# A long convolution with a routed expert: one stage's matmuls made with 128 moving columns instead of 256

## The chip, the cores and the metric

The kernel runs on one core of a Trainium2 chip. The metric is the device time of one execution in microseconds (us), of which the median of three runs is taken. Five engines work beside each other: PE (TensorE: matmuls, with its weight loads shown apart as PEld), DVE (VectorE), ACT (ScalarE), POOL (GpSimd) and SP (SyncE, which issues DMAs).

## What is computed

Two steps, for 8 sequences ("units" here, 0 to 7) of 6336 positions and 128 channels, all in float32:

```python
# step 1: causal convolution along the sequence, by Fourier transforms
Xf = np.fft.rfft(x, n=2*S, axis=1)
Hf = np.fft.rfft(h, n=2*S, axis=0)
y  = np.fft.irfft(Xf * Hf[None], n=2*S, axis=1)[:, :S, :]
# step 2: in each sequence the 128 positions with the highest score go through an expert
scores = np.einsum('bsd,d->bs', y, w_gate)
out = y.copy()
for b in range(B):
    top = np.argpartition(-scores[b], 128)[:128]
    xe = y[b, top]
    g = 1 / (1 + np.exp(-scores[b, top]))
    out[b, top] = xe + g[:, None] * (np.maximum(xe @ w1, 0) @ w2)
```

The change touches step 1 alone.

## The kernel before, in words

The sequence is cut as 50 x 128 (`N1` = 50, `N2` = 128), and the transform is done by matmuls against tables, in four stages for each unit:

- **a** (`stage_a`, matmuls on line 194): the products over the 50, out of the loaded input blocks; ACT or DVE copies the result to `reg[unit % 2]`. The two buffers of `reg` are `big` (even units) and `reg` (odd units).
- **b** (`stage_b`, matmuls through the helper `by_halves`, line 109): the products over the 128 (called n2), one for each of the 50 values of k. The 50 are taken in 13 chunks, `KCH`: twelve of 4 and one of 2. A chunk's weights `wt` come from HBM (`load_b`, tile `wbuf`, for units 6 and 7 partly `big`). The moving operand `rows_of(unit, k)` is 128 x 256 of `reg`: 128 pairs of neighbouring floats, each pair 100 floats behind the last. The results of four k fill a pair of PSUM banks (`pt`, 128 x 1024); there are two such pairs (`pairs`), used in turn. DVE multiplies them with the filter's spectrum (lines 276 and 282, two outputs, one of them in place of the input in `reg`), and POOL adds the parts (line 287).
- **c** (`stage_c`, line 300): the inverse products over the 128, 64 moving columns each, 64 matmul calls in one call of the stage; ACT copies them out to `half` (line 301).
- **d** (`stage_d`, line 320): the inverse products over the 50, 128 moving columns each, read out of `half` as 64 pairs of neighbouring floats, each pair 256 floats behind the last. ACT and DVE combine the results (lines 324, 329, 330), POOL multiplies them with the gate's weights (line 338), and SP sends them to HBM.

`by_halves` cuts a product by its 128 output rows: it issues two matmuls, one with weight columns 0 to 63 and one with 64 to 127, with the same moving operand, which write the partitions 0 to 63 and 64 to 127:

```python
for lo in range(0, n, 64):
    hi = min(lo + 64, n)
    nc.tensor.matmul(out[lo:hi], w[:, lo:hi], r, **k)
```

The order of all work is written out by hand (`manual_schedule`, the list `plan`). First come the filter and unit 0: stage a of both, then the "j" steps, which make the filter's spectrum (`stage_h`) and do stage b of unit 0. From then on two kinds of stretch alternate: c of unit u merged with b of unit u+1 (two calls of c, then two chunks of b, and so on; seven such stretches, of units 1 to 7 in b), and d of unit u merged with a of unit u+2. DVE's share of the search for the 128 best positions (`search`) is spread over both; for units 6 and 7 the experts follow at the end, whose products also go through `by_halves`, with 128 contiguous moving columns (line 645).

Of the kernel before, what the change touches and what calls it, by code (L numbers as in the profile page):

```python
# [33 lines left out]
def conv_moe(ctx, tc, x, h, w_gate, w1, w2, fa_d, wb_d, wc_d, at_d, tri_d, cst_d, outs):  # L34
# [19 lines left out]
    def pair():  # L54
        return turn(pairs)
# [8 lines left out]
    def wide(name):  # L64
        return tp.tile([128, 1024], F32, tag="t", name=name, bufs=5)
# [39 lines left out]
    def by_halves(out, w, r, **k):  # L105
        n = out.shape[0]
# [3 lines that stand above are left out]
# [115 lines left out]
    def rows_of(unit, k):  # L225
        return reg[(unit + 2) % 2].rearrange("p (j k t) -> p j k t", k=N1, t=2)[:, :, k]
# [33 lines left out]
    def stage_b(unit, c, tabs):  # L260
        wt, ht = tabs
        k0, kn = KCH[c]
        pt = pair()
        for k in range(kn):
            by_halves(pt[:, k * 256:k * 256 + 256], wt[:, k], rows_of(unit, k0 + k), start=True, stop=True)
        pt = pt[:, 0:kn * 256]
        rv = reg[unit % 2].rearrange("p (h a j k t) -> p h a j k t", h=2, a=4, k=N1, t=2)[:, :, :, :, k0:k0 + kn]
        tx = wide("tx")[:, 0:kn * 256]
        tv = tx.rearrange("p (h a j k t) -> p h a j k t", h=2, a=4, k=kn, t=2)
        if unit >= SINGLE:  # L270
            src = pt.rearrange("p (z r b x) -> p b z r x", r=2, b=2, x=32)
            for b in range(2):
                for w, dst in zip(ht, (rv, tv)):
                    o = dst.rearrange("p h a j k t -> p (h a) j k t")[:, 4 * b:4 * b + 4].rearrange("p a j k t -> p k a j t")
                    f = w[:, b].rearrange("p (z x) -> p z x", x=32).unsqueeze(2).broadcast_to([128, 2 * kn, 2, 32])
                    v.tensor_tensor(out=o, in0=src[:, b], in1=f, op=ALU.mult)
        else:
            src = pt.rearrange("p (k h a j t) -> p k h a j t", h=2, a=4, j=16, t=2)
            for w, dst in zip(ht, (rv, tv)):
                w = w.rearrange("p (k h j t) -> p k h j t", h=2, j=16, t=2)  # L280
                w = w.unsqueeze(3).broadcast_to([128, kn, 2, 4, 16, 2])
                v.tensor_tensor(out=dst.rearrange("p h a j k t -> p k h a j t"), in0=src, in1=w, op=ALU.mult)  # L282
        h = 4 if unit >= SINGLE else 2
        yv = reg[unit % 2].rearrange("p (h r j z) -> p h r j z", h=h, r=2, z=2 * N1)[:, :, :, :, 2 * k0:2 * (k0 + kn)]
        zv = tx.rearrange("p (h r j z) -> p h r j z", h=h, r=2, z=2 * kn)
        for r in range(2):
            g.tensor_tensor(out=yv[:, :, r], in0=yv[:, :, r], in1=zv[:, :, 1 - r], op=ALU.add if r else ALU.subtract)  # L287
# [525 lines left out]
    for s in plan:  # L813
        kind, unit = s[0], s[1]
# [30 lines left out]
        elif kind == "j":  # L845
# [12 lines left out]
            if early:  # L858
                spectra.append(join())
            stage_b(0, c, (tabs.pop(s)[0], [st[:, 0:n], st[:, n:2 * n]]))  # L860
            if join and not early:
                spectra.append(join())
            if s[2] < 8:
                load_x(16 + s[2])
            if s[2] in (2, 4, 6, 8):
                fold_to(15 + s[2] // 2)
        elif kind == "b":
            stage_b(*s[1:], tabs.pop(s))
            if unit == SINGLE and s[2] in (9, 11):
                load_x((unit + 2) * 8 + s[2] // 2 + 1)  # L870
# [161 lines left out]
```

## Time and profile before

| | |
|---|---|
| runs | 797.77, 797.80, 798.41 us; median 797.8 us |
| profiled execution | 804.7 us, of which the trace's span is 802.8 us |
| granted TensorE clock, mean | 0.983 of full speed |
| PE busy | 735.0 us (92%) |
| PEld busy | 643.2 us (80%) |
| DVE busy | 629.7 us (78%) |
| POOL busy | 551.3 us (69%) |
| ACT busy | 451.5 us (56%) |

"Busy" is the time in which at least one instruction of that engine is under way. A matmul call of float32 shows as two records of PE and two of PEld. Matmul records overlap, so the mean duration of one is longer than the step from one to the next; a step has to be worked out from the length of a row and the number of records in it. "The chain" is the work that ended last, followed back from the last instruction to what released each step.

### The profile page before, as it was taken

Reading aid. Unit: us, or ns where it says so; the run is one execution under the profiler, and the core shown is the slowest. Engines: PE = TensorE matmul, PEld = TensorE weight load, DVE = VectorE, ACT = ScalarE, POOL = GpSimd, SP = SyncE. Lnnn points to the kernel's source line nnn. Section 1 sums busy time; section 2 is a strip of 40 time slices with the busy share of each in tenths; the row PEclk is TensorE's granted clock in tenths of the full one; section 3 lists DMA queues with packets and bytes.
Section 4 is the critical chain, followed back from the end, with each engine's and each line's share of the span. In section 5 each row is a group of like instructions: output and inputs, shape, how many; then the busy total and the mean of one; then the engine's idle time right before and its main releaser. Section 6 shows DMA issues by size and latency. Waiting matters only on the chain.

```text
span 802.8 us, 39710 instructions
## 1 busy us (share of the span) xinstructions
PE 735.0 (92%) x17566; PEld 643.2 (80%) x17566; DVE 629.7 (78%) x1067; ACT 451.5 (56%) x965; POOL 551.3 (69%) x406
## 2 busy tenths in 40 slices
PE   6699979999999999999999999999999998888665
PEld 6675578888999878987889788889888888778554
DVE  5549956676767699999877898999668997975983
ACT  4687643365336546666456466655554666655562
POOL 0018928977797779877978698777885666722933
PEclk9889989999999999999999999999999999999989
DMA  7829816657865776578647774699478736521610
GB/s 268 259 83 329 267 55 215 208 166 233 261 216 160 231 261 215 155 219 273 229 126 230 256 259 123 193 331 327 126 224 267 253 110 183 171 65 31 205 54 17
DMA packets 82292, 157.64 MB, mean 196 GB/s; under 512 B 9366, under 2 KB 30088, under 8 KB 82120
## 3 DMA queue, kind: packets, MB, share of 16 engines
q1 hardware_dynamic: 81224, 154.05, 59.4%
q8 instruction: 138, 2.26, 1.1%
q0 software_dynamic: 896, 1.05, 0.5%
q14 instruction: 34, 0.28, 0.1%
HBM read 121.77 MB, written 33.29 MB: 193 GB/s over the span
## 4 chain that ended last, share of the span: by engine, by line
PE 65%; DVE 18%; issue 7%; DMA 5%; ACT 2%; POOL 1%; SPq 1%; another core or an unknown queue 0%; POOLq 0%; DVEq 0%; ACTq 0%
PE pb L300 23%; PE pt L109 17%; PE pb L320 10%; PE pt L194 10%; DVE tx L282 2%; DVE cmp L464 2%; PE pb L109 2%; PE pb L194 1%; PE pm L109 1%; DVE ss L354 1%; DVE st L329 1%; DVE st L330 1%; DMA out<-st 1%; ACT junk L477 1%; DVE st L251 1%
## 5 line engine op out<-in xcount | busy, mean ns | idle before, releaser
L301 ACT COPY half<-pb 114x512 f32<-114x512 f32 x224 | 147.0, 656 | 165.5 <-PE pb L300 161.1
L287 POOL TENSOR_TENSOR big<-big,tx 128x512 f32<-128x512 f32 (+1 forms) x104 | 132.0, 1302 | 77.5 <-DVE tx L282 68.0
L338 POOL TENSOR_TENSOR tm<-st,wg 114x1024 f32<-114x1024 f32 x56 | 133.8, 2392 | 63.4 <-DVE st L330 41.7
L287 POOL TENSOR_TENSOR reg<-reg,tx 128x512 f32<-128x512 f32 (+1 forms) x104 | 130.8, 1291 | 48.2 <-PE pb L300 28.5
L300 PE MATMUL pb<-wc,reg 128*50 128x64 f32 x4096 | 126.4, 220 | 4.1 <-issue 3.7
L300 PEld LDWEIGHTS pb<-wc,reg 128*50 128x50 f32 x4096 | 121.8, 126 | 7.7 <-issue 5.7
L300 PEld LDWEIGHTS pb<-wc,big 128*50 128x50 f32 x4096 | 118.5, 126 | 3.0 <-ACT reg L211 0.3
L300 PE MATMUL pb<-wc,big 128*50 128x64 f32 x4096 | 120.6, 219 | 0.1
L320 PE MATMUL pb<-half,wbuf 114*50 114x128 f32 x1792 | 112.2, 274 | 5.7 <-issue 2.1
L320 PEld LDWEIGHTS pb<-half,wbuf 114*50 114x50 f32 x1792 | 97.1, 123 | 12.9 <-issue 3.2
L109 PE MATMUL pt<-big,wbuf 128*64 128x256 f32 x704 | 87.4, 388 | 0.8 <-issue 0.6
L109 PE MATMUL pt<-reg,wbuf 128*64 128x256 f32 x704 | 85.1, 388 | 0.0
L211 ACT COPY reg<-pt 128x800 f32<-128x800 f32 x64 | 56.3, 928 | 44.4 <-PE pt L194 44.3
L282 DVE TENSOR_TENSOR tx<-pt,wbuf 128x1024 f32<-128x1024 f32 (+1 forms) x65 | 76.3, 1174 | 0.0
L329 DVE TENSOR_TENSOR st<-pb,st 114x512 f32<-114x512 f32 x56 | 38.6, 689 | 47.4 <-PE pb L320 32.4
L109 PEld LDWEIGHTS pt<-big,wbuf 128*64 128x64 f32 x704 | 57.7, 135 | 19.5 <-issue 1.1
L109 PEld LDWEIGHTS pt<-reg,wbuf 128*64 128x64 f32 x704 | 52.3, 135 | 20.9
L211 ACT COPY big<-pt 128x800 f32<-128x800 f32 x59 | 51.6, 931 | 22.6 <-PE pt L194 20.7
L356 DVE TENSOR_REDUCE ss<-tm 114x16 f32<-114x1024 f32 x48 | 58.4, 1216 | 7.2 <-POOL tm L338 6.5
L282 DVE TENSOR_TENSOR reg<-pt,wbuf 128x1024 f32<-128x1024 f32 (+1 forms) x39 | 45.9, 1178 | 18.6 <-PE pt L109 18.4
L194 PE MATMUL pt<-fa,big 50*64 50x100 f32 x2336 | 59.4, 249 | 0.0
L194 PEld LDWEIGHTS pt<-fa,big 50*64 50x64 f32 x2336 | 51.9, 133 | 6.3 <-issue 3.5
(175 smaller groups left out, 1206.0 us busy)
## 6 DMA issues: line engine op xcount, KB each, us to landing
wbuf<-tab_at SPq DMA_DIRECT2D x128, 200.0 KB
out<-st SPq DMA_DIRECT2D x112, 200.0 KB
wbuf<-tab_wb SPq DMA_DIRECT2D x84, 256.0 KB
wbuf<-hd SPq DMA_DIRECT2D x84, 256.0 KB
big<-in_x SPq DMA_DIRECT2D x37, 512.0 KB
half<-in_x SPq DMA_DIRECT2D x15, 512.0 KB
hd<-st SPq DMA_DIRECT2D x24, 256.0 KB
reg<-in_x SPq DMA_DIRECT2D x12, 512.0 KB
```

The source lines that it names most:

```text
L109: nc.tensor.matmul(out[lo:hi], w[:, lo:hi], r, **k)
L194: nc.tensor.matmul(o, w, tab[lanes, c], start=True, stop=True)
L211: nc.scalar.copy(out=o, in_=i)
L282: v.tensor_tensor(out=dst.rearrange("p h a j k t -> p k h a j t"), in0=src, in1=w, op=ALU.mult)
L287: g.tensor_tensor(out=yv[:, :, r], in0=yv[:, :, r], in1=zv[:, :, 1 - r], op=ALU.add if r else ALU.subtract)
L300: nc.tensor.matmul(pt[i2 * 64:i2 * 64 + N1, o:o + HD], w, wc[:, i2], start=True, stop=True)
L301: nc.scalar.copy(out=hv[0:LN, c * 4 + j:c * 4 + j + 2].rearrange("p j r m t -> p (j r) t m"), in_=pt[0:LN].rearrange("p (j t m) -> p j t m ...
L320: nc.tensor.matmul(pt[r][a * 64:a * 64 + N1, c * 128:c * 128 + 128], ats[c // 2][0:LN, c % 2, a, r], hv[0:LN, :, r, m], start=True, stop=True)
L329: v.tensor_tensor(out=st[:, 0:512], in0=pt[1][0:LN], in1=st[:, 512:1024], op=ALU.add)
L338: e.tensor_tensor(out=tm[:, o:o + z].rearrange("p (a d) -> p a d", d=n), in0=st[:, o:o + z].rearrange("p (a d) -> p a d", d=n), in1=w.unsq ...
L356: v.tensor_reduce(out=ss[u][:, :, :, 4 * i:4 * i + 4].rearrange("p b s c -> p s c b"), in_=tm.rearrange("p (s c b d) -> p s c b d", s=2, c ...
L464: v.tensor_tensor(out=cv, in0=cur.unsqueeze(2).broadcast_to([LN, nb, nv, HD]), in1=nth[:, :, 0:nv].unsqueeze(3).broadcast_to([LN, nb, nv, ...
```

## The change

In `stage_b` each product of a k is made in two halves of 128 moving columns (64 pairs of neighbouring floats), one after the other, in place of one of 256. Each half goes through `by_halves`, so the same weights are loaded for either half. Outputs, their places in PSUM, the chunks, the order of stages and everything after the products are as before.

```diff
         for k in range(kn):
-            by_halves(pt[:, k * 256:k * 256 + 256], wt[:, k], rows_of(unit, k0 + k), start=True, stop=True)
+            for z in range(2):
+                o = k * 256 + z * 128
+                by_halves(pt[:, o:o + 128], wt[:, k], rows_of(unit, k0 + k)[:, 64 * z:64 * z + 64], start=True, stop=True)
```

## Rows read from the trace of the kernel before

**Rows 1.** The page: busy time by engine, and the chain by engine.
```profile
PE 735.0 (92%) x17566; PEld 643.2 (80%) x17566; DVE 629.7 (78%) x1067; ACT 451.5 (56%) x965; POOL 551.3 (69%) x406
...
PE 65%; DVE 18%; issue 7%; DMA 5%; ACT 2%; POOL 1%; SPq 1%; another core or an unknown queue 0%; POOLq 0%; DVEq 0%; ACTq 0%
```

**Rows 2.** Stretches: length, busy us (instructions) by engine, PEclk, DMA share, GB/s.
```profile
50.00:100.00 50.00, 46.82 (x528) 29.87 (x528) 47.44 (x57) 37.44 (x79) 39.81 (x32) 1.00 0.80 272
...
115.90:167.40 51.50, 51.50 (x1228) 43.85 (x1232) 33.86 (x30) 20.25 (x31) 42.90 (x34) 1.00 0.60 198
...
359.20:412.70 53.50, 53.03 (x1264) 45.32 (x1258) 48.08 (x66) 27.99 (x67) 47.74 (x38) 1.00 0.65 213
...
608.70:661.60 52.90, 51.78 (x1236) 44.47 (x1232) 49.59 (x99) 30.04 (x76) 33.27 (x27) 1.00 0.67 216
```

**Rows 3.** The chain within the seven c-and-b stretches, by line, in order.
```profile
by line: PE pb L300 54.3%; PE pt L109 42.8%; ACT reg L211 2.5%; PE pt L194 1.2%; issue 0.1%
...
by line: PE pb L300 55.3%; PE pt L109 44.7%; PE pt L194 0.4%; PE pb L320 0.1%
...
by line: PE pb L300 47.4%; PE pt L109 28.9%; DMA wbuf<-tab_wb 7.6%; DVE tx L282 4.5%; ACT junk L477 3.4%; issue 2.5%; DVE reg L282 2.2%; DVE cmp L464 1.6%; PE pb L320 1.0%; PE pt L194 0.4%; PE pm L109 0.4%; DVE pm L454 0.4%; ACT bias L470 0
...
by line: PE pb L300 47.2%; PE pt L109 31.8%; DVE tx L282 3.5%; ACT junk L477 3.4%; issue 3.3%; DVE big L282 2.3%; DVE ss L356 2.1%; PE pm L109 1.6%; DVE cmp L464 1.5%; PE pm L535 0.9%; PE pt L194 0.6%; PE pb L320 0.4%; DVE pm L454 0.3%; DVE
...
by line: PE pb L300 40.8%; PE pt L109 29.0%; DMA wbuf<-tab_wb 6.9%; DVE tx L282 4.4%; ACT junk L477 3.4%; issue 2.9%; DVE reg L282 2.2%; DVE ss L356 2.2%; SPq L359 1.6%; DVE cmp L464 1.6%; DVE st L329 1.3%; DVE st L330 1.3%; PE pb L320 0.7%
...
by line: PE pb L300 41.7%; PE pt L109 37.9%; issue 7.2%; DVE tx L276 6.0%; DVE big L276 4.9%; DVE reg L133 1.6%; PE pm L535 1.0%; PE pb L320 0.6%; PE pm L109 0.6%; POOLq L133 0.1%; POOL big L287 0.1%; DVE reg L134 0.1%; POOLq L287 0.0%
...
by line: PE pb L300 43.5%; PE pt L109 31.8%; DMA big<-hd 7.3%; DMA big<-in_moe_w 5.1%; SPq L162 4.1%; ACT junk L477 3.3%; issue 1.6%; PE pb L320 1.6%; DVE cmp L464 1.5%; DVE reg L276 1.4%; DVE tx L276 1.2%; SPq L156 0.6%; PE pm L109 0.4%; D
```

**Rows 4.** Pieces of the chain: start us, us, what.
```profile
144.91 3.57 PE pb L300 x128
148.49 3.63 PE pt L109 x32
```

**Rows 5.** Groups of PE by form: count | busy us, mean ns | idle before.
```profile
L109 PE MATMUL pt<-big,wbuf 128*64 128x256 f32 x704 | 87.4, 388 | 0.8 <-issue 0.6
L109 PE MATMUL pt<-reg,wbuf 128*64 128x256 f32 x704 | 85.1, 388 | 0.0
...
L109 PE MATMUL pt<-big 128*64 128x256 f32 x96 | 12.7, 388 | 0.0
...
L109 PE MATMUL pt<-reg,big 128*64 128x256 f32 x96 | 12.0, 388 | 0.0
```

**Rows 6.** Timelines of matmul bursts: start us, us, engine, line, names, form, count.
```profile
141.56 2.90 PE L109 MATMUL pt<-reg,wbuf 128*64 128x256 f32 x24
...
144.74 3.75 PE L300 MATMUL pb<-wc,big 128*50 128x64 f32 x128
...
169.23 1.37 PE L320 MATMUL pb<-half,wbuf 114*50 114x128 f32 x22
...
172.54 1.60 PE L320 MATMUL pb<-half,wbuf 114*50 114x128 f32 x26
...
736.10 1.59 PE L109 MATMUL pt<-half 128*64 128x128 f32 x26
```

**Rows 7.** Timelines of weight loads: start us, us, engine, line, names, form, count.
```profile
149.00 2.64 PEld L109 LDWEIGHTS pt<-reg,wbuf 128*64 128x64 f32 x24
...
736.21 1.35 PEld L109 LDWEIGHTS pt<-half 128*64 128x64 f32 x24
```

**Rows 8.** Durations: min/median/max ns of line 109; mean of lines 300 and 320.
```profile
L109 PE MATMUL pt<-half x64: 272/273/312, 726.4 to 737.6; 128*64 128x128 f32 x64
...
L300 PE MATMUL pb<-wc,big 128*50 128x64 f32 x4096 | 120.6, 219 | 0.1
L320 PE MATMUL pb<-half,wbuf 114*50 114x128 f32 x1792 | 112.2, 274 | 5.7 <-issue 2.1
```

**Rows 9.** Waits in 115.9 to 167.4: who, for whom, us, times, longest.
```profile
DVE reg L282 <- PE pt L109: 17.6, 6, 4.7
```

## The prediction

> **What bounds the kernel now.** The page comes first: PE is busy 92% of the span, and the chain that ended last lies 65% on PE, 18% on DVE, 5% on DMA [rows 1]. An average doesn't say what the changed matmuls are worth, so the stretches in which they run come next. There are eight: unit 0's (the "j" steps, about 50 to 100 us) and seven in which stage c of one unit is merged with stage b of the next. In three of these seven that stand for all, PE is busy 51.5 of 51.5, 53.0 of 53.5 and 51.8 of 52.9 us, while DVE is busy 33.9, 48.1 and 49.6 and POOL 42.9, 47.7 and 33.3 [rows 2]. So PE sets their length, with DVE close behind it where a search runs beside them. Unit 0's stretch is different: DVE is busy 47.4 of 50 us, PE 46.8 [rows 2], and its chain alternates between the engines.
>
> The third view is the chain inside the seven stretches. In the first two it is only line 300 (stage c) and line 109 (stage b), in turn: 3.57 us for 128 records of c, then 3.63 us for 32 records of b, with nothing between them [rows 3, 4]. In the others some 12 us at the start lie on other things: a table's DMA, DVE's products, and the first round of the search. Line 109's share, times the length of each window (53, 51.4, 53, 54, 53, 53 and 54 us), is 22.7 + 23.0 + 15.3 + 17.2 + 15.4 + 20.1 + 17.2 = 131 us [rows 3]. That is the time on which the change works and which sets the end.
>
> **The change part by part.** The matmuls concerned are 704 + 704 + 96 + 96 = 1600 records with 256 moving columns, 200 for each of 8 units [rows 5]. They run two at a time, one in each column half of the array, so I count in pairs: 800 pairs, and 100 in a full stretch. After the change there are 3200 records of 128 columns, 1600 pairs, and as many weight loads.
>
> First, the price of a pair now. A row of a burst lasts (number of pairs - 1) steps and the duration of the last record. For 24 records in 2.90 us, with 388 ns for one, that is (2900 - 388) / 11 = 228 ns [rows 5, 6]; the chain gives 3630 / 16 = 227 ns [rows 4]. I take 227.
>
> Second, the price of a pair with 128 columns. The trace has no 128-column pair on these operands, but two neighbours. (i) The experts' products on the same line, with the same 128 rows, the same 64 weight columns and new weights each time, only with contiguous moving columns: 26 records in 1.59 us, 273 ns each, (1590 - 273) / 12 = 110 ns [rows 6, 8]. (ii) Stage d, line 320, whose moving operand is also 64 pairs of neighbouring floats with a gap between, though 114 rows and 50 weight columns: (1370 - 274) / 10 = 110 ns and (1600 - 274) / 12 = 110.5 ns [rows 6, 8]. So neither the gaps in the moving operand nor the wider weights cost anything that these rows show at 128 columns. I take 110 for the new pair, 220 for what was 227.
>
> Why should two halves cost less than the whole? The steps say so without a cause. Stage c, 64 columns: (3750 - 219) / 63 = 56 ns [rows 6, 8]. From 64 to 128 columns the step grows by 54, or 0.84 ns a column; at that slope 256 columns would take 110 + 108 = 218. They take 227: there is an excess of 9 to 10 ns in the long pair that no shorter one has. On what it hangs, the trace does not tell, and that gives the bounds. If it hangs on the length of the instruction, halves don't have it: 220, or 7 ns less per old pair. If it belongs to these columns as such (pairs of floats 100 floats apart, where stage d's are 256 apart), each half keeps half of it: 110 + 5 = 115, 230, or 3 ns more. If it is a fixed price of an instruction on this operand, each half pays it in full: 110 + 9.5 = 119.5, 239, or 12 ns more. I choose the first, because row (ii) is the nearest in shape and shows nearly none of the excess, which it should if reading pairs of floats caused it.
>
> The granted clock is 1.00 in all the rows of stretches that bear on this [rows 2], the level of 2.4 GHz, so the excess is no matter of the clock. At that level the Trainium skill ("TensorE: Matmul & The Clock Gate", the section "Wait — 56ns, not 53.3ns?") has one matmul follow another by its columns at one a cycle and about 2.5 ns whatever the length. Estimated from that with two cycles a column for a float32 record, the steps would be 55.8, 109.2 and 215.8 ns. The rows at 64 and 128 columns agree, and the one at 256 (227) does not; by this rule alone doubling the instructions can only add, 2.5 ns per old pair.
>
> Third, the weight loads. They double, and each takes 134 to 137 ns, longer than the 110 ns step. Now they follow at (2640 - 135) / 11 = 228 ns a pair and leave gaps; in the experts' burst at (1350 - 137) / 11 = 110 ns a pair, two or more under way at once [rows 7]. What hides them is the stream of the matmul before. If that cover failed, a pair would take its load's 137 ns at least: 274 for 227, 47 / 227 of 131 us, 27 us more. The experts' row excludes this for the same weights, and stage c, whose step is half as long, loads weights for each of its matmuls too.
>
> Fourth, what is late next. A full stretch gets shorter by 100 x 7 ns = 0.7 us of some 52. DVE has 52.9 - 49.6 = 3.3 us left in the fullest stretch shown, POOL 53.5 - 47.7 = 5.8 [rows 2]. In the first stretch DVE itself waits 17.6 us for line 109's results [rows 9]. So neither takes over. The number of PSUM banks, the chunks' order and the DMA queue's order stay, and DMAs have a third of each stretch free [rows 2], so tables come forward with the work that frees their buffers. In unit 0's stretch I count nothing: DVE bounds it. Its whole value would be 100 pairs x 7 ns = 0.7 us.
>
> Sum: 131 us x 7 / 227 = 4.0 us. The profiled execution took 804.7 us, so it would take 800.7. It is 0.9% above the median of the runs, 797.8, and scaled to that the prediction is 797.8 x 800.7 / 804.7 = 793.8 us. The likeliest case's own range goes from all eight stretches gaining at the best step (1600 x 109 against 800 x 227 ns, 7.2 us: 790.6) to a gain of 2 us (795.8).
>
> **Rivals.**
>
> (A) The excess belongs to the columns, and each extra pair pays the small fixed part besides: 230 for 227, 131 x 3 / 227 = 1.7 us more, 799.5 us. For it: the step of the 256-column pairs is about 227 in every burst, and nothing in the trace reads pairs of floats 100 apart in a shorter instruction. Against it: stage d. The skill's fixed 2.5 ns per matmul points the same way, with 1.4 us more by the same sum.
>
> (B) The slower one: the excess is a fixed start-up price of an instruction on this operand. It is paid by PE in stage b of the seven stretches: 239 for 227, 131 x 12 / 227 = 6.9 us more, 804.7 us. It decides as soon as the new pair takes over 113.5 ns, half of 227; there the result turns from faster to slower. Against it: rows (i) and (ii) show no such price, and the weights and the output form are those of (i).
>
> (C) The products get faster and the stretches do not, since what now ends just after PE (DVE with the search, tables' DMAs at the start of a stretch, the d-and-a stretches behind) takes the time up: 797.8 us. For it: in four of the seven stretches a quarter to a third of the chain's line-109 time is already replaced by other waits [rows 3]. Against it: the first two stretches, 46 us of the 131, have no other wait at all.
>
> (D) The weight loads don't stay hidden: 27 us more, 825 us; excluded as far as rows 7 go.
>
> **How the numbers follow.** Forecast 0.53, A 0.20, B 0.10, C 0.14, D 0.03. A difference under about 0.2%, 1.6 us, cannot be told from none in this kernel. Faster by more than that (below 796.2): the forecast, 0.53. Within it: C, and A for somewhat over half, 0.27. Slower (above 799.4): the rest of A, B and D, 0.20. The range of 8 in 10 takes in the forecast's own from 791 on, C and A, and leaves out B and D: 791 to 801.
>
> **What would show it.** In the changed profile the groups of line 109 have 128 columns and twice the records, with a mean near 275 ns in place of 388; 64 records of two chunks take about 3.5 us on the chain in place of 3.63; the weight loads of these groups follow without gaps at 110 ns a pair. Line 109's share of the chain falls by some 4 us in the seven stretches, and stage c's rows stay at 3.57. A pair's step of 115 or of 119 ns would show A or B, and a step of 110 with an unchanged end C. The prediction is wrong if the step is over 113.5 ns, or if stretches that PE filled show new idle time before line 109 or line 300.

## The result and the profile after

The changed kernel takes 804.1 us (median of 6 runs, 803.0 to 811.1) against 798.1 for the kernel before (6 runs, 795.5 to 800.0). The ratio is 1.0104 with a 95% interval of 1.007 to 1.0138: about 1% slower, where 793.8 us had been forecast. The profiled execution took 811.1 us, its span is 809.3 us; it is the longest of the six (the other five: 803.0 to 807.0), as the profiled one of the kernel before, 804.7 us, lies above all of that kernel's six.

The page of the changed kernel, answering [rows 1 and 5], with the instruction queue, one group of stage c and the two large groups of line 109:

```profile
PE 741.5 (92%) x19166; PEld 699.7 (86%) x19166; DVE 627.2 (77%) x1067; ACT 451.4 (56%) x965; POOL 551.0 (68%) x406
...
q8 instruction: 150, 2.46, 1.2%
...
PE 65%; DVE 18%; issue 7%; DMA 5%; ACT 2%; POOL 1%; SPq 1%; POOLq 0%; DVEq 0%; ACTq 0%
...
L302 PE MATMUL pb<-wc,big 128*50 128x64 f32 x4096 | 122.4, 219 | 2.4 <-issue 2.3
...
L109 PE MATMUL pt<-big,wbuf 128*64 128x128 f32 x1408 | 88.0, 276 | 1.7 <-issue 1.5
L109 PE MATMUL pt<-reg,wbuf 128*64 128x128 f32 x1408 | 86.8, 276 | 1.0 <-DMA wbuf<-tab_wb 0.7
```

The records of line 109 have 128 columns and 276 ns, and there are as many as the change says. The chain by engine looks as before; the page announces the loss only by idle time put down to "issue", time in which the engine waited for nothing that the profile shows: 2.3 us before this group of stage c, which had 0.1 us of idle time in all [rows 8], and 1.5 us before line 109 on `big`, which had 0.6 [rows 5]. (Lines after the changed one stand two further down: stage c is line 302, DVE's product 284.)

The stretches, answering [rows 2]: length, busy time of PE, PEld, DVE, ACT and POOL with their instructions, granted clock, DMA share, GB/s. Three of the seven c-and-b stretches are left out, the sum is over all seven.

```profile
113.40:167.20 53.80, 52.11 (x1426) 51.65 (x1426) 33.91 (x31) 20.25 (x31) 44.26 (x35) 1.00 0.59 190
...
360.50:415.40 54.90, 53.90 (x1464) 52.89 (x1460) 48.46 (x67) 28.14 (x67) 49.30 (x38) 1.00 0.67 213
...
527.80:585.00 57.20, 54.80 (x1468) 53.19 (x1464) 49.38 (x92) 28.13 (x67) 43.81 (x34) 1.00 0.77 260
616.60:670.90 54.30, 52.67 (x1439) 51.96 (x1435) 50.60 (x101) 31.15 (x78) 34.41 (x28) 1.00 0.68 216
sum 382.50, PE 370.68 PEld 365.36 DVE 316.99 ACT 188.11 POOL 310.16; mean PE 52.95 PEld 52.19 DVE 45.28 ACT 26.87 POOL 44.31
```

The same sum for the kernel before:

```profile
sum 369.80, PE 365.20 PEld 320.26 DVE 316.06 ACT 187.68 POOL 304.19; mean PE 52.17 PEld 45.75 DVE 45.15 ACT 26.81 POOL 43.46
```

The seven stretches together are 12.7 us longer. DVE has hardly more work in them than before (317.0 for 316.1 us), the clock is 1.00, and PE, which filled the first stretch (51.5 of 51.5), leaves 1.7 of 53.8 us empty. What is outside of them, 426.8 us, was 433.0 before; but single executions of the experiments below have 424 to 431 us there, and the changed kernel's second one (`after_again`) 430.5, so these 6.2 us belong to no step of the change that could be shown.

The chain inside the first stretch, answering [rows 3 and 4]: its shares by line, then pieces with start, length, what.

```profile
by line: PE pb L302 50.1%; PE pt L109 41.9%; issue 3.0%; PE pt L194 2.8%; PE pb L322 2.2%
...
120.88 3.57 PE pb L302 x128
124.45 3.64 PE pt L109 x64
...
135.31 1.22 PE pb L302 x42
136.53 1.30 issue
137.83 2.60 PE pb L302 x85
140.44 2.36 PE pt L109 x41
142.79 0.36 issue
143.15 1.53 PE pt L109 x22
```

Two calls of stage c take 3.57 us as before and two chunks of stage b 3.64 for 3.63, until PE stops in the middle of 128 equal instructions of stage c, none of which waits for anything new. The instruction queue (q8) shows what happened just before. Packets, MB and share of the DMA queues: first from 126.8 to 135.6 us, then from 135.6 to 136.7 us.

```profile
q1 hardware_dynamic: 827, 2.03, 70.8%
...
q1 hardware_dynamic: 138, 0.25, 60.5%
q8 instruction: 1, 0.02, 5.5%
```

For 8.8 us no instruction packet starts, then one that is under way for 5.5% of 16 engines in 1.1 us, 0.97 us, to about 136.6. PE goes on at 137.83, 1.2 us after it. One more packet lies at 140.6 to 141.7; PE's second stop ends at 143.15.

How much each round needs (two calls of c and two chunks of b are called a round from here on, some 7.2 us): the kernel before has 35,132 records of PE and PEld and this on q8:

```profile
q8 instruction: 138, 2.26, 1.1%
```

That is 64 bytes a record, so a packet of 16 KB holds 256; the change adds 3,200 records and 12 packets. A round took 128 + 32 matmul records (a call of c is 32 matmul calls, 64 records, and not 64 calls as said above) and as many weight loads, 320 records; it now takes 128 + 64 and as many loads, 384 records, 1.5 packets.

The waits of PE's weight loads over the seven stretches: who, for whom, us in total, times, longest. The changed kernel:

```profile
PEld pb L302 <- issue: 6.7, 11, 1.4
...
PEld pt L109 <- issue: 4.3, 6, 1.1
```

The kernel before:

```profile
PEld pt L109 <- issue: 1.1, 1, 1.1
...
PEld pb L300 <- issue: 0.3, 2, 0.2
```

So 11.0 us for 1.4: 9.6 of the 12.7 us are stops without a named wait.

The whole trace bears out that these stops are waits for packets. Of the 14 waits that last 0.3 us or more, 13 end 1.2 to 1.6 us after a 16 KB packet has landed (the other one 2.5 us). They also come one packet of records apart: at the three that end at 212.6, 219.2 and 224.3 us, PE and PEld have started 9,582, 9,836 and 10,092 records since the start of the trace, and one packet has landed between each and the next. The second execution (`after_again`) stops elsewhere at times, but where both stop in the same place, it is at the same count of records: 5,762, 22,570, 27,918, 28,174 and 30,968.

### The profile page after: what moved, and what is told of

Read it like the earlier page. It is cut to its first block, busy times and chain, and to the rows that moved or that the text cites. A ratio compares the mean times of both kernels' runs of the same rounds, so it can differ in the third digit from the quotient of the medians.

```text
span 809.3 us, 42909 instructions
## 1 busy us (share of the span) xinstructions
PE 741.5 (92%) x19166; PEld 699.7 (86%) x19166; DVE 627.2 (77%) x1067; ACT 451.4 (56%) x965; POOL 551.0 (68%) x406
## 3 DMA queue, kind: packets, MB, share of 16 engines
q8 instruction: 150, 2.46, 1.2%
## 4 chain that ended last, share of the span: by engine, by line
PE 65%; DVE 18%; issue 7%; DMA 5%; ACT 2%; POOL 1%; SPq 1%; POOLq 0%; DVEq 0%; ACTq 0%
PE pb L302 23%; PE pt L109 18%; PE pb L322 10%; PE pt L194 10%; DVE tx L284 2%; DMA out<-st 2%; DVE cmp L466 2%; PE pb L194 1%; DVE st L251 1%; DVE ss L356 1%; PE pb L109 1%; DVE st L331 1%; ACT junk L479 1%; PE pm L109 1%; DVE st L332 1%
## 5 line engine op out<-in xcount | busy, mean ns | idle before, releaser
L302 PE MATMUL pb<-wc,big 128*50 128x64 f32 x4096 | 122.4, 219 | 2.4 <-issue 2.3
L109 PE MATMUL pt<-big,wbuf 128*64 128x128 f32 x1408 | 88.0, 276 | 1.7 <-issue 1.5
L109 PE MATMUL pt<-reg,wbuf 128*64 128x128 f32 x1408 | 86.8, 276 | 1.0 <-DMA wbuf<-tab_wb 0.7
L109 PEld LDWEIGHTS pt<-big,wbuf 128*64 128x64 f32 x1408 | 81.8, 135 | 4.4 <-issue 1.9
L109 PEld LDWEIGHTS pt<-reg,wbuf 128*64 128x64 f32 x1408 | 80.6, 135 | 1.8 <-issue 1.1
```

What stands on the lines that cost most here:

```text
L302: nc.tensor.matmul(pt[i2 * 64:i2 * 64 + N1, o:o + HD], w, wc[:, i2], start=True, stop=True)
```

## The experiments

**Theory 1**: PE runs out of instructions, because 384 records for 7.2 us are more than its queue brings in time beside the other transfers. **Theory 2**: the loss belongs to the doubled records themselves (their loads, their reads), whatever else PE has to fetch; some expectations below set the doubled weight loads apart as Theory 3. All ratios are against the kernel before, run beside them.

**Fewer instructions in stage c.** `y_c128` is the changed kernel, `x_c128` the kernel before, both with this edit, half as many calls of 128 columns:

```diff
                     for r in range(2):
                         w = yv[:, n // 16, r, c // 8, n % 16, :, t]
-                        o = ((i * 2 + r) * 2 + t) * HD
-                        for i2 in range(2):
-                            nc.tensor.matmul(pt[i2 * 64:i2 * 64 + N1, o:o + HD], w, wc[:, i2], ...)
+                        o = (i * 2 + t) * 2 * HD
+                        nc.tensor.matmul(pt[r * 64:r * 64 + N1, o:o + 2 * HD], w,
+                                         wc.rearrange("p c m -> p (c m)"), start=True, stop=True)
```

> The changed kernel, and stage c besides made with half as many matmul calls of twice the length: one call moves all 128 columns of the table for a set of weights, with the output halves now the two values of r, where two calls moved 64 columns each. Left out: the order of rows that stage d needs, so the output is not the convolution; PE's busy time of stage c is about the same (64 pair steps of 56 ns, 3.58 us, become 32 of 110 ns, 3.52 us), its PE instructions in a call of two halve from 256 to 128. Theory 1 (instruction supply: PE runs out of fetched instructions because the c-and-b stretches now issue 384 where they issued 320 per 7.2 us): the unnamed stalls of PE in these stretches, 9 to 10 us in the changed kernel, go nearly away, and the time falls from 804.1 to 795 to 798 us, ratio to the kernel before 0.995 to 1.001. Theory 2 (the new pair costs 114 ns, 228 for 227, and that with a scatter of the runs is all): ratio 1.005 or above, within 1 us per thousand of the changed kernel's 1.010, since nothing of stage b's price changes. Theory 3 (twice the weight loads hold PE up): half of stage c's loads go too, so a fall like theory 1's is possible, but it would show as longer steps and not as stalls.

> The kernel before, with stage c made with half as many calls of twice the length, as in y_c128; left out is the order of rows that stage d needs. Theory 1 (instruction supply): the kernel before has few such stalls in the c-and-b stretches, 1 to 2 us in all, so at most 1 to 2 us are won beside 7 x 0.5 us of stage c's own shorter steps: ratio 0.993 to 0.999, and the difference between y_c128 and this one falls to the price of the pairs alone, 0 to 2 us. Theory 2 (pairs and scatter): the same ratio here, but y_c128 stays 6 us above this one. Theory 3 (weight loads): a ratio like theory 1's, and y_c128 2 to 3 us above.

`y_c128`: 794.1 us, 0.9909 (0.9878 to 0.994), a little below what Theory 1 expected; `x_c128`: 796.6 us, 0.9933 (0.9905 to 0.9961). A round now needs 256 and 192 records. The seven stretches sum to 368.5 and 368.7 us, and the stops are gone from both. `y_c128`:

```profile
PEld pb L301 <- issue: 0.3, 2, 0.2
PEld pt L109 <- issue: 0.2, 1, 0.2
```

`x_c128`:

```profile
PEld pb L299 <- issue: 0.3, 2, 0.2
```

With the same doubled records of stage b, the change costs nothing as soon as stage c leaves room in the instruction stream (the two ratios differ by 0.0024, their intervals overlap). Theory 2 falls. Stage c itself hardly shortens, 3.49 us for two calls in `y_c128` for 3.57.

**More instructions.** `e_64` cuts the products into four parts (shown against the changed kernel):

```diff
-            for z in range(2):
-                o = k * 256 + z * 128
-                by_halves(pt[:, o:o + 128], wt[:, k], rows_of(unit, k0 + k)[:, 64 * z:64 * z + 64], ...)
+            for z in range(4):
+                o = k * 256 + z * 64
+                by_halves(pt[:, o:o + 64], wt[:, k], rows_of(unit, k0 + k)[:, 32 * z:32 * z + 32], ...)
```

> Stage b's products in four parts of 64 moving columns, the weights loaded four times; the result is the same. Theory 1 (instruction supply): stage b issues 256 PE instructions where it issued 64 in a pair of chunks, so a stretch needs 512 per 7.2 us, and the stalls of PE grow well over those of the changed kernel: 812 to 830 us, ratio 1.018 to 1.04. Theory 2 (the price goes by columns): four steps of 57 ns are 228, as two of 114 are, so the time is the changed kernel's, 802 to 806 us, ratio 1.005 to 1.01. Theory 3 (weight loads): the step grows over 57 ns, and the time by 131 us x that growth; the stalls stay as they are.

871.5 us, 1.0836 (1.076 to 1.0912), far more than expected. The step of a pair is 58 to 59 ns (92 records in 2.70 us on its chain), four of them 236 for 227, which is some 5 us (131 x 9 / 227). Most of the rest is stops (waits of the weight loads; then line 109's idle time before its records, by form):

```profile
PEld pt L109 <- issue: 38.8, 32, 3.2
PEld pb L302 <- issue: 15.0, 21, 1.8
```

```profile
L109 PE MATMUL pt<-reg,wbuf 128*64 128x64 f32 x2816 | 94.8, 223 | 19.7 <-issue 19.7
```

At 512 records for a round the stops are 53.8 us: 320 records give 1.4 us, 384 give 11.0, 512 give 53.8. The loss grows much faster than the count. All 42 stops of 0.3 us or more in these stretches end 1.1 to 1.6 us after a packet has landed. Price and stops are 58 of the 68 us by which the seven stretches grow (437 us for 369.5, from the first to the last record of each); the other 10 stand in no row here.

**No halves.** `e_full` loads 128 weight columns at once, so that 16 records stand for 16 pairs; a round needs 288 records:

```diff
-            by_halves(pt[:, k * 256:k * 256 + 256], wt[:, k], rows_of(unit, k0 + k), start=True, stop=True)
+            nc.tensor.matmul(pt[:, k * 256:k * 256 + 256], wt[:, k], rows_of(unit, k0 + k), start=True, stop=True)
```

> The other direction: stage b's products of a k in one call with all 128 weight columns and 256 moving columns, without the cut in halves; the result is the same. The number of PE instructions of stage b halves against the kernel before. Theory 1 (instruction supply) expects fewer stalls than before, up to 2 us less in the c-and-b stretches, if one call costs what the two halves cost (454 ns for a k). Theory 2 expects only the price of the call: two records of 128 weight columns one after the other at two cycles a column are 2 x 217 = 434 ns for 454, 131 us x 20 / 454 = 5.8 us less, ratio 0.993; if a record of 128 weight columns takes four cycles a column, 870 ns, 120 us more, ratio 1.15.

815.5 us, 1.0176 (1.0133 to 1.0218), slower for a reason of its own, not for want of instructions; none of the prices expected came. Pieces of its chain:

```profile
116.43 3.85 PE pt L265 x16
120.28 3.71 PE pb L300 x128
```

Against [rows 4] both pieces are longer, by 0.22 and 0.14 us, though the step of a record inside the burst is 225 to 228 ns. The time lies at the switches between 128 and 50 weight columns: from the start of the last record of line 265 to the first of line 300 it is 315 ns. 0.36 us for each of some 6.5 rounds is 2.3 us a stretch; the seven sum to 383.0, 1.9 us more each than before.

**Fewer bytes beside the same instructions.** If the packets come late because they share the DMA engines with data, less data should bring them in time. `a_q` (the changed kernel), `b_q` (before) and `e_64q` (four parts) load a quarter of stage b's tables in units 1 to 5:

```diff
-        nc.sync.dma_start(out=wt[:, 0:kn], in_=wb_d[:, k0:k0 + kn])
+        ln = 1 if 0 < unit < SINGLE else kn
+        nc.sync.dma_start(out=wt[:, 0:ln], in_=wb_d[:, k0:k0 + ln])
...
-        nc.sync.dma_start(out=ht, in_=hd[unit % 2, :, k0 * 128:(k0 + kn) * 128])
+        nc.sync.dma_start(out=ht[:, 0:ln * 128], in_=hd[unit % 2, :, k0 * 128:(k0 + ln) * 128])
```

> The changed kernel, with the tables of stage b loaded to a quarter in units 1 to 5 (output not the convolution); its control is b_q. Theory 1b (fetches stand behind data): the five stretches lose the stalls, 53.8 to 54.8 us become 51.5 to 52.5 and the kernel is within 2 us of b_q, the price of the pairs; ratio to the kernel before 0.985 to 1.0. Theory 1a (a fetch's own time): 5 to 7 us above b_q, as the changed kernel is above the one before.

> The kernel before with the same tables loaded to a quarter in units 1 to 5 (output not the convolution): the control for a_q, showing what fewer bytes bring by themselves. The waits for a table at the start of the stretches of units 3 and 5 (4 us each on the chain) go, other waits follow close behind: 790 to 798 us, ratio 0.985 to 0.999, under either theory.

> The kernel with four parts of 64 columns (e_64), and in units 1 to 5 the two tables of stage b loaded to a quarter only (the rest of their tiles is what an earlier chunk left there, so the output is not the convolution). PE's instructions are those of e_64 to the last; the DMA bytes of the tables in the five stretches fall from 512 KB to 128 KB a chunk. Theory 1b (a block of instructions comes late because its fetch stands behind data in the DMA engines): the stretches of units 1 to 5, 60 to 63 us in e_64, fall by 4 us or more each, those of units 6 and 7 stay at 63 to 64; in all 20 us or more less than e_64's 871, ratio 1.03 to 1.06. Theory 1a (a fetch has its own time, and PE keeps too few instructions in store at this rate): the five stretches stay within 2 us of e_64's, ratio 1.07 to 1.09.

`a_q`: 803.7 us, 1.0041 (1.0007 to 1.0075); `b_q`: 799.1, 0.9974 (0.9943 to 1.0006). In the five stretches with smaller loads the two agree within 0.2 us apart from one of 0.8 us in which `a_q` is the shorter. The window of 196 to 248 us (columns as in the stretches above) of the changed kernel, of `a_q` and of `b_q`:

```profile
196.00:248.00 52.00, 49.52 (x1337) 49.07 (x1334) 33.96 (x30) 19.00 (x29) 44.57 (x35) 1.00 0.68 218
```

```profile
196.00:248.00 52.00, 52.00 (x1444) 51.49 (x1442) 37.41 (x33) 21.55 (x33) 45.87 (x37) 1.00 0.45 133
```

```profile
196.00:248.00 52.00, 52.00 (x1230) 44.07 (x1229) 36.36 (x32) 21.66 (x33) 47.19 (x37) 1.00 0.45 134
```

At a DMA share of 0.45 in place of 0.68 PE doesn't stop any more in this window, with all its 384 records a round. Its weight loads are those of the changed kernel to the last, so twice the loads don't hold PE up by themselves, and Theory 3 falls too. The two kernels' totals still lie 4.6 us apart, not within 2 as expected: 2.8 us are in unit 6's stretch (56.8 for 54.0 us), whose loads were not cut. `e_64q` went only part of the way: 849.1 us, 1.0609 (1.0548 to 1.067); its five stretches are 8.2, 1.8, 3.5, 2.4 and 4.8 us shorter than those of `e_64`, the two uncut ones not. In the window of 196 to 248 us its DMA share is 0.43, that of `e_64` 0.73. So data traffic delays the packets, but at 512 records it isn't all that limits them; what the rest is stays open.

**What the excess of 227 over 216 to 218 ns hangs on.** `e_flat256` (from the kernel before) and `e_flat128` (from the changed one) read the moving operand from a constant table without gaps:

```diff
-            by_halves(pt[:, k * 256:k * 256 + 256], wt[:, k], rows_of(unit, k0 + k), start=True, stop=True)
+            by_halves(pt[:, k * 256:k * 256 + 256], wt[:, k], tri.rearrange("p c n -> p (c n)"), start=True, stop=True)
```

> The kernel before, but stage b's products read as moving operand 256 contiguous floats of a constant table in place of the pairs of floats 100 apart of the unit's data (so the output is not the convolution). Theory P (the excess of the long pair over the slope from 64 to 128 columns comes with reading pairs of floats 100 apart): the pair step falls from 227 to 218 ns, line 109 on the chain by 131 x 9 / 227 = 5 us, ratio 0.992 to 0.995. Theory L (it comes with the length of the instruction): the step stays at 225 to 227 ns, ratio 0.998 to 1.002.

> The changed kernel's two halves of 128 columns, but read from 256 contiguous floats of a constant table, as in e_flat256 (output not the convolution). The price of a pair is then the same by columns in both: 2 steps of 109 ns for one of 216, 2 ns more, 131 us x 2 / 216 = 1 us. Instruction supply: the stalls come all the same, since the instructions are as many, so it is 5 to 9 us above e_flat256 (ratio 0.993), at 0.999 to 1.004. Price alone: 1 us above e_flat256, ratio 0.993 to 0.996.

Timelines of `e_flat256`, then of `e_flat128` (start, us, what):

```profile
122.71 2.98 PE L109 MATMUL pt<-tri,wbuf 128*64 128x256 f32 x26
```

```profile
124.75 2.46 PE L109 MATMUL pt<-tri,wbuf 128*64 128x128 f32 x42
```

By the prediction's way of counting, (2980 - 379) / 12 = 217 ns and (2460 - 273) / 20 = 109 ns. The long pair on the table without gaps has no excess: it comes with the operand that is read, not with the length. Two halves gain nothing against 217. `e_flat256` takes 796.1 us, 0.993 (0.9897 to 0.9963); `e_flat128` 809.2, 1.0078 (1.0043 to 1.0112). Here the halving alone, at equal time per column, costs 1.5%, more than expected, and the waits show where (the trace of `e_flat128` is of an execution of 812.0 us). `e_flat256`:

```profile
PEld pb L300 <- issue: 0.9, 4, 0.4
PEld pt L109 <- issue: 0.6, 1, 0.6
```

`e_flat128`:

```profile
PEld pb L302 <- issue: 10.8, 13, 1.9
...
PEld pt L109 <- issue: 2.9, 6, 1.5
```

`e_gap` (from the kernel before; a single execution, of which only the steps are read) takes the pairs of units 3 and 5 at four distances:

```diff
-            by_halves(pt[:, k * 256:k * 256 + 256], wt[:, k], rows_of(unit, k0 + k), start=True, stop=True)
+            mv = rows_of(unit, k0 + k)
+            if unit in (3, 5):
+                gap = (100, 96, 64, 128)[c % 4]
+                mv = big[:, 0:128 * gap].rearrange("p (j s) -> p j s", s=gap)[:, :, 0:2]
+            by_halves(pt[:, k * 256:k * 256 + 256], wt[:, k], mv, start=True, stop=True)
```

> The kernel before, but in units 3 and 5 stage b reads its 128 pairs of floats from the other buffer at gaps that change from chunk to chunk: 100 floats (as now), 96, 64 and 128 (output not the convolution; the chunks may wait for other work, so only the steps within a burst are read). If the excess of 10 ns over 216 comes with any pair of floats that stands alone, all four gaps show 225 to 228 ns. If it comes with the gap itself, 100 shows 226 and at least one of the round gaps 216 to 220, as stage d's pairs 256 floats apart show nearly none of it (110 for 109).

Its timeline, for distances of 100, 96, 64 and 128 floats:

```profile
274.61 1.53 PE L109 MATMUL pt<-big,wbuf 128*64 128x256 f32 x12
...
276.19 2.11 PE L109 MATMUL pt<-big,wbuf 128*64 128x256 f32 x16
...
281.98 1.90 PE L109 MATMUL pt<-big,wbuf 128*64 128x256 f32 x12
...
288.78 2.83 PE L109 MATMUL pt<-big,wbuf 128*64 128x256 f32 x12 [4.62 <-POOL big L134]
```

The first three steps are about 228, 241 and 289 ns (last records of 388, 420 and 453). The fourth row gives 440 ns (last record of 628) and can't stand beside them: PE had been idle for 4.62 us before it, and the granted clock was 0.50, the level of 1.2 GHz, where the other three ran at 1.00. Two more chunks of unit 5 tell the clock from the distance, the first at 128 floats, the second at 100 (their rows, then the granted clock, third from the end, in the window of the fourth row above and in theirs):

```profile
496.82 2.51 PE L109 MATMUL pt<-big,wbuf 128*64 128x256 f32 x16 [2.32 <-POOL big L134]
...
506.93 2.83 PE L109 MATMUL pt<-big,wbuf 128*64 128x256 f32 x12 [3.97 <-POOL big L134]
```

```profile
288.80:292.00 3.20, 3.20 (x16) 1.83 (x18) 0.00 (x0) 0.00 (x0) 2.40 (x2) 0.50 0.25 73
...
496.90:498.90 2.00, 2.00 (x16) 1.05 (x18) 0.00 (x0) 0.00 (x0) 1.93 (x2) 1.00 0.45 118
506.90:510.20 3.30, 3.27 (x16) 1.91 (x18) 0.00 (x0) 0.00 (x0) 0.00 (x0) 0.50 0.00 0
```

At 1.00 the distance of 128 takes (2510 - 454) / 7 = 294 ns, about as much as 64; at 0.50 the distance of 100 takes the same (2830 - 628) / 5 = 440 as that of 128. Over all chunks of the two units that ran at 1.00, the median step from start to start is 227 to 232 ns at 100 floats, 248 to 252 at 96, 286 to 287 at 64 and 288 at 128. Neither expectation had this: at the full clock the distance itself sets the price, from 5% over 217 at 100 floats to a third at 64 and 128. That stage d's pairs, 256 floats apart, show nothing of it [rows 6, 8] stays unexplained; they differ in rows, weight columns and in reading another buffer, and none of these was tried.

**The changed kernel once more**, `after_again`, without an edit:

> The changed kernel once more, beside the kernel before and the two runs below on one chip. If the stalls of PE are its own (instruction supply) and not those of one execution: ratio 1.005 to 1.012, and in its trace the seven c-and-b stretches are 8 to 14 us longer in sum than the 370 us of the kernel before, with the steps inside bursts at 114 and 56 ns. If the first comparison was scatter: 0.998 to 1.004.

811.3 us, 1.0115 (1.0068 to 1.0162). Its seven stretches sum to 379.3 us, with stops of 6.6 and 3.0 us before lines 302 and 109: the loss repeats, within some 3 us.

## Why the prediction was wrong

**The price of a pair now, 227: right.**

**"The price of a pair with 128 columns": wrong in size.** It took 110. The trace of the changed kernel (start, us, what; matmuls, then weight loads) says:

```profile
149.74 1.88 PE L109 MATMUL pt<-reg,wbuf 128*64 128x128 f32 x30
```

```profile
149.87 1.61 PEld L109 LDWEIGHTS pt<-reg,wbuf 128*64 128x64 f32 x27
```

(1880 - 275) / 14 = 114.6 ns, and 3.64 us / 32 = 114 on the chain: 228 for 227, so that the term is 131 x 1 / 227 = 0.6 us lost and not 4.0 gained. The step that failed is the choice of row (ii), stage d, as nearest in shape: "pairs with a gap" was taken as one kind of operand, and the distance of the pairs, 256 against 100, was held to be without effect. `e_flat256` and `e_gap` show that the excess hangs on the distance; what spares stage d, whose pairs lie further apart still, stays open. It goes with the columns, as in rival A, whose 230 was a little high.

**The weight loads: right.** They follow at (1610 - 135) / 13 = 113 ns, 134 ns each, hidden behind the matmuls. Rival D is out.

**"What is late next": wrong, and this is the larger term.** It went through DVE, POOL, PSUM banks, queues and tables, and that held nearly: in the seven stretches PE's weight loads wait 0.9 us for DVE's products and PE 0.7 us for a table, which they didn't before. It left out what PE itself consumes, its instruction stream, which the change raises from 320 to 384 records for 7.2 us. 9.6 us of new stops and 0.6 us of price are 10.2 of the 12.7 us by which the stretches grew; the two waits just named may be part of the other 2.5, and no row names the rest. Since the stretches of `y_c128` are no longer than those of `x_c128`, they should go with the supply too, but that isn't shown. The kernel before had a small sign: 0.6 us of "issue" before line 109 [rows 5]. It is one stop, whose weight load resumes at 536.5 us, 1.2 us after a packet has landed. The 7% of "issue" on its chain [rows 1] is no such sign: `y_c128`, without these stops, has 7% too.

Two of the prediction's own conditions named this outcome: a step over 113.5 ns, and new idle time before lines 109 and 300. Both came: 114.6 ns, and the stops. The end, 804.1, lies beside rival B's 804.7 by luck, not by its mechanism: a price of 239 for a pair isn't there, and no rival was the instruction supply.

The Trainium skill ("Runtime: NRT & Kernel Launch", section "Instruction fetch mechanics") says that an engine's instructions come in blocks of 16 KiB, 256 instructions, fetched ahead over a queue of its own, at a cost that is mostly hidden. The size agrees (2.46 MB in 150 packets). That the cost is mostly hidden agrees with the kernel before, 1.4 us of stops, and less and less with 11.0 us here and 53.8 us in `e_64`; the measurement decides.

**Scaling to the median: it came out, but by luck.** The profiled execution lies 0.9% above the median in the changed kernel as in the one before (811.1 / 804.1, 804.7 / 797.8). In `after_again`, the same kernel, the profiled execution (811.6) lies at the median (811.3), so the 0.9% belongs to single executions.

## What to carry to other kernels

On an engine that is busy all the time, count its instructions for each microsecond of the stretch, weight loads included, beside the DMA traffic there: an equal amount of work in more instructions isn't free, and half as many instructions for equal work in stage c took 0.7% off the kernel before (`x_c128`), though whether stage c can be written so with its results where stage d wants them was not tried. Idle time put down to "issue" in the middle of a burst of equal instructions, with a late packet on the instruction queue before its end, is the sign. And take the price of a strided operand only from a row with the same stride, and compare steps only at the same granted clock.

## What the runs showed of the hardware

- TensorE's stops of 0.3 us or more without a named wait end 1.1 to 1.6 us after a 16 KB packet of instructions has landed (13 of 14 in the changed kernel, 42 of 42 in `e_64`). Over the same seven stretches all such stops sum to 1.4, 11.0 and 53.8 us at 320, 384 and 512 records for 7.2 us; smaller loads beside them, which cut the DMA share of a window from 0.68 to 0.45, remove them at 384 and not at 512.
- At a granted clock of 1.00 a float32 pair of records of 256 columns takes 217 ns on a table without gaps; made of two neighbouring floats each, it takes 228 ns at 100 floats distance, about 241 at 96, 289 at 64 and 294 at 128. At a clock of 0.50 both 100 and 128 take 440. The Trainium skill ("Advanced Engine Details and Errata", section "SBUF Cachelines") says that it takes at least two hits on a 16-byte line to absorb the memory's latency. Each pair of floats here is two such hits, and the distance between the pairs still sets the time.
- Going from 128 to 50 weight columns costs about 90 ns over the step (315 ns for 225); both ways together 0.36 us for a round.
